# Row-tiled attention work in units of four heads of one row half, two units side by side in two sets of three PSUM banks

## The chip, the cores and the metric

The program runs on one core of a Trainium2 chip. The metric is the device time of one launch in microseconds, lower is better; the median of the runs of a kernel stands for it.

## What is computed

The reference is one pre-norm transformer block in float32 over S = 2048 rows of width D = 640: causal attention with 32 heads of width 20 over a window of 256 keys, an output projection with a residual, then a gated feed-forward of width 1536 with a residual.

```python
qkv = layernorm(x) @ wqkv                       # 32 heads, Dh = 20
scores = einsum("bhqd,bhkd->bhqk", q, k) * Dh ** -0.5
mask = (i - j >= 0) & (i - j < 256)
p = softmax(where(mask, scores, -1e9))
h = x + einsum("bhqk,bhkd->bhqd", p, v) @ wo
h2 = h + (gelu(layernorm(h) @ w_gate) * (layernorm(h) @ w_up)) @ w_down
```

## The kernel before

**Tiling.** The rows are cut into 16 blocks of 128, two blocks to a chunk for the q and k projections. A block's window is at most three key blocks: the one two blocks back (only keys later than the query's place in it count), the one before it (all), and its own (only keys up to the query). The float32 products of the projections are made of three float16 products (high by high, high by low, low by high). Scores are made twice. First q·k with the query on the output's partitions gives each row's maximum (`maxima`, 60 contraction rows; `max_out`). The maxima go back into two more contraction rows of qT (`max_rows`, `max_transpose`), and the second product with the key on the partitions (`scores`, 62 rows) comes out with the maximum subtracted, ready for the exponential (`score_out`) and for the product with v (`value_lane`).

**Row tiling.** 60 or 62 contraction rows fill less than half of TensorE's 128 rows. qT and kT hold one head of a pair on partitions 0 to 63 and the other on 64 to 127 (`par`), and a matmul on each half is issued as a pair. In the page the queries' product is `ra` or `rb` <- kT,qT and the keys' product is `ra` or `rb` <- qT,kT. The value product is column tiled: four heads in four groups of 32 output columns, into one bank that is held throughout (`pv`).

**PSUM.** The eight banks are five rings: two banks `mm` for all dense products, two `ra` and two `rb` for the row-tiled work, one `pv`, one `tp` for transposes. One step of `row_lane` takes one pair of heads of the maxima into one ring and one pair of the scores into the other, or only one of the two where the other is not ready (`row_need`, `two`). Each bank then has its own reader: VectorE reads a head's 128x384 scores with the mask added and takes the maximum (`tensor_tensor_reduce`, the custom instruction `junk` <- `ra`,`mask`, followed by a read of the accumulator into `mxs`), ScalarE takes the exponential of a head's 128x384 into `pt`. When four heads of `pt` are there, GpSimd zeroes the masked corners with two affine selects, and the value product may run.

**Order.** All instructions are emitted in an order that the program works out while it builds itself. `Clock` holds an estimated time for each engine and each buffer, `cost` an estimated price of each instruction, and the loop at the end of `block_kernel` takes, at each moment of that clock, the first lane that can start: outputs of banks first, then transposes, then side work (layernorm, weight splitting, loads), then attention lanes and the dense lane in an order that depends on which of the two is behind. On the chip each engine runs its list in order, and waits on semaphores.

**Stages.** At the start x, wq, wk and wv are loaded by SyncE's queue, the first blocks are normalised (`x_lane`) and the weights scaled and split. The first NR = 4 blocks are turned by TensorE; the others are cast (`sph`, `spl`) and turned by a DMA transpose. The q and k of a chunk leave through DRAM (`qk_out`, `qk<-qks`) and come back in the stacked form (`stack`, `qT<-qk`, `kT<-qk`). Two constant rows of kT are filled by DMA from `big`. Dense work (`dense_lane`: `qk`, `vproj`, `wo_block`, then the first part of the feed-forward) stands between the row-tiled steps. When the last block has left attention, the feed-forward runs alone.

Of the kernel before, what the change touches and what calls it, by code (L numbers as in the profile page):

```python
# [4 lines left out]

# [5 lines left out]
F32 = mybir.dt.float32  # L11
# [10 lines left out]
P = 128  # L22
# [11 lines left out]
SWITCH = 0.095  # L34
NEG = -1.0e30
# [7 lines left out]
ME = 15  # L43
# [7 lines left out]
class Clock:  # L51
# [97 lines left out]
    def others(self, ap, eng):  # L149

        return max([0.0] + [end + self.LAT for _, e, end in self.rd.get(ap.tensor.name, ())
                            if e != eng])

    def issue(self, eng, cost, reads, writes, move=False):
# [8 lines left out]
        if move:  # L163
            self.t[eng] = start + 0.4
# [10 lines left out]
class Engine:  # L175
# [4 lines left out]
    def __getattr__(self, op):  # L180
        real = getattr(self.real, op)

        def call(*args, **kw):
# [5 lines left out]
            if op in ("memset", "affine_select"):  # L189
                ins = out if op == "affine_select" else []  # L190
            self.clock.issue(self.name, self.cost(op, out[0], ins), ins, out,
                             op.startswith("dma_start"))
# [4 lines left out]
    def cost(self, op, out, ins):  # L197
# [20 lines left out]
        if self.name == "vector":  # L218
            m = max([n] + [i.free_size() for i in ins])
            if op == "tensor_copy" and half or op == "tensor_scalar" and m > 320:  # L220
                return (0.065 if half else 0.185) + 0.00053 * m
# [12 lines left out]
def block_kernel(ctx: ExitStack, tc: tile.TileContext, x, wqkv, wo, wg, wu, wd, out):  # L234
# [10 lines left out]
    banks = dict(mm=2, ra=2, rb=2, pv=1, tp=1)  # L245
# [3 lines left out]
    def bank(name, dt=F32):  # L249
        opened[name] += 1  # L250
        return nc.tile(psum, [P, 512 if dt == F32 else 1024], dt, name, banks[name])

    def ps_tp(dt=F32):
        return bank("tp", dt)

    def done(name):
        opened[name] -= 1
# [10 lines left out]
    NR = 4  # L268
# [5 lines left out]
    LEAD, TARGET = 20, 0.0  # L274
# [5 lines left out]
    def need(*reads, slots=(), when=None, eng="tensor"):  # L280

        def f():
            if when and not when() or any(opened[n] >= banks[n] for n in slots):
                return INF
            return max([nc.ready(reads, eng)]
                       + [nc.slot(psum, n, banks[n]) for n in slots])
# [28 lines left out]
    class Weight:  # L315
# [34 lines left out]
        def scale(self, lane, tp="tp"):  # L350
# [22 lines left out]
            done(tp)  # L373
# [99 lines left out]
    def transpose_part(src, hi, lo, c0, c1, tp="tp"):  # L473
# [10 lines left out]
        done(tp)  # L484
# [5 lines left out]
    def products(n, term, ready=None, at_=None):  # L490
# [5 lines left out]
        def start(i):  # L496
            if ready and not ready(i) or not ps and opened["mm"] >= banks["mm"]:
                return INF
            t = nc.ready([x for ab in term(i) for x in ab], "tensor")
            return t if ps else max(t, nc.slot(psum, "mm", banks["mm"]))  # L500
# [17 lines left out]
    def ff_scales(fg):  # L518
# [6 lines left out]
        nc.vector.tensor_tensor(ffk[:, fg, 3:4], pw[:, us:us + 1], pw[:, gs:gs + 1], op=ALU.mult)  # L525

    def ff_scales_down(fg):
        ds_ = C_D + fg
        nc.vector.tensor_scalar(ffk[:, fg, 2:3], ffk[:, fg, 3:4], pw[:, ds_:ds_ + 1],
                                _pow2(-WE - XE - UE - WE - WE), op0=ALU.mult, op1=ALU.mult)  # L530

# [13 lines left out]
    mask = wp.tile([P, 3 * P], F32, name="mask")  # L545
    nc.gpsimd.memset(mask, 0.0)
    nc.gpsimd.affine_select(mask[:, 0:P], mask[:, 0:P], pattern=[[1, P]], compare_op=ALU.is_ge,
                            fill=NEG, base=-1, channel_multiplier=-1)
# [794 lines left out]
```

## Time and profile before

| | |
|---|---|
| runs | 1103.23, 1106.27, 1107.80 us; median 1106.27 |
| span of the profiled execution, first to last instruction | 1095.7 us |
| around it (median of the runs minus the span) | 10.6 us |
| busy: TensorE / VectorE / ScalarE / GpSimd | 1023.9 / 662.5 / 452.0 / 176.4 us |
| mean granted TensorE clock over the span | 0.975 |

The profiled execution has no time of its own beside its span; 10.6 us is what the runs' median lies above it, and is taken as what surrounds the span. In a row of the trace the first number is the start or the group's busy time, as the sentence ahead of it says; PE is TensorE (PEld its weight loads), DVE VectorE, ACT ScalarE, POOL GpSimd, SP SyncE. All instructions carry the line of one helper (L184 before, L192 in the changed kernel), so they are told apart by their tiles. Matmul durations contain the pipeline's depth; their pace is read from start to start.

### The profile page before, as it was taken

The page shows a single profiled execution, that of the slowest core. Times are in us where ns is not written, and L with a number is a line of the kernel's source. Part 1 is how long each engine was busy: PE and PEld are TensorE (multiplying, and loading weights), DVE is VectorE, ACT ScalarE, POOL GpSimd, SP SyncE. Part 2 cuts the span into 40 slices and gives each one's busy share as a digit, 9 for nine tenths or more (in the row PEclk, how much of TensorE's full clock was granted, in tenths as well). Part 3 has the DMA queues.
Part 4 walks back from the last instruction along what each step waited for, and adds up shares of the span by engine and source line. Part 5 has one row for each costly group of instructions (what it writes and reads, how often), then busy time and mean ns, then how long its engine had stood idle before and what let it go on. Part 6 is the DMA issues. An engine that isn't in the chain of part 4 may idle for free.

```text
span 1095.7 us, 24693 instructions
## 1 busy us (share of the span) xinstructions
PE 1023.9 (93%) x9902; PEld 611.4 (56%) x9902; DVE 662.5 (60%) x1949; ACT 452.0 (41%) x860; POOL 176.4 (16%) x286
## 2 busy tenths in 40 slices
PE   5469899899899999999999999999999999999998
PEld 3335556566566666666554564455455555545546
DVE  8667898788686776766679739942522263222323
ACT  3213555566555766656667773411210111110110
POOL 1001112233233333323332320000000000000000
PEclk9779899899999999999999999999999999999999
DMA  6546739446253251322442114410400040001001
GB/s 240 142 91 145 205 106 203 99 97 141 63 131 90 66 128 53 94 76 70 87 150 87 42 40 154 121 25 36 109 1 1 3 124 19 1 1 49 1 1 48
DMA packets 122774, 91.41 MB, mean 83 GB/s; under 512 B 65636, under 2 KB 101732, under 8 KB 121700
## 3 DMA queue, kind: packets, MB, share of 16 engines
q1 hardware_dynamic: 99556, 79.09, 28.1%
q10 hardware_dynamic: 23104, 10.75, 3.8%
q8 instruction: 77, 1.26, 0.5%
q14 instruction: 37, 0.30, 0.1%
HBM read 54.07 MB, written 20.97 MB: 68 GB/s over the span
## 4 chain that ended last, share of the span: by engine, by line
PE 73%; DVE 9%; DMA 8%; ACT 4%; issue 3%; ACTq 1%; SPq 1%; POOL 0%; DVEq 0%; POOLq 0%
PE mm L184 58%; PE pv L184 6%; PE rb L184 4%; DVE junk L184 4%; PE ra L184 4%; ACT pt L184 3%; DMA qk<-qks 3%; DMA kT<-qk 2%; PE tp L184 1%; DMA xh<-sph 1%; DMA ol<-spl 1%; DVE am L184 1%; ACTq L184 1%; DMA xt<-in_x_dram 1%; DVE qks L184 1%
## 5 line engine op out<-in xcount | busy, mean ns | idle before, releaser
L184 POOL TENSOR_SCALAR_AFFINE_SELECT pt<-pt 128x512 f32<-128x512 f32 x240 | 154.4, 666 | 387.1 <-ACT pt L184 384.6
L184 DVE CUSTOM_DVE_ANT_0 junk<-ra,mask 128x384 bf16<-128x384 f32 (+2 forms) x260 | 136.9, 527 | 61.3 <-PE ra L184 40.5
L184 ACT ACTIVATE pt<-ra,esc 128x384 f32<-128x384 f32 (+2 forms) x260 | 131.9, 560 | 90.6 <-PE ra L184 75.5
L184 DVE CUSTOM_DVE_ANT_0 junk<-rb,mask 128x384 bf16<-128x384 f32 (+2 forms) x252 | 134.5, 534 | 57.4 <-PE rb L184 33.1
L184 ACT ACTIVATE pt<-rb,esc 128x384 f32<-128x384 f32 (+2 forms) x252 | 128.0, 560 | 79.3 <-PE rb L184 63.8
L184 DVE SCALAR_TENSOR_TENSOR gel<-mm,ffk,gel 128x512 f32<-128x512 f32 x48 | 36.0, 749 | 143.7 <-PE mm L184 143.6
L184 ACT ACTIVATE gel<-mm,ffk 128x512 f32<-128x512 f32 x48 | 33.0, 687 | 190.9 <-PE mm L184 190.9
L184 PE MATMUL pv<-pt,v 128*21 128x128 f32 x2880 | 106.4, 279 | 1.6 <-ACT oT L184 1.5
L184 DVE SCALAR_TENSOR_TENSOR ht<-mm,ffk,ht 128x320 f32<-128x320 f32 x96 | 52.8, 550 | 81.9 <-PE mm L184 81.8
L184 PEld LDWEIGHTS <-ah 128*128 128x128 f16 x768 | 74.9, 98 | 31.0 <-issue 0.4
L184 ACT CAST ah<-gel 128x512 f16<-128x512 f32 x48 | 29.7, 618 | 131.0 <-DVE gel L184 131.0
L184 PEld LDWEIGHTS pv<-pt,v 128*21 128x21 f32 x2880 | 69.4, 101 | 17.6 <-ACT oT L184 2.5
L184 PEld LDWEIGHTS <-qT 60*128 60x128 f16 x640 | 27.1, 93 | 92.4 <-issue 84.6
L184 PEld LDWEIGHTS <-kT 62*128 62x128 f16 x1440 | 60.9, 96 | 31.8 <-issue 20.7
L184 PEld LDWEIGHTS <-gu 128*128 128x128 f16 x480 | 45.6, 98 | 53.5 <-issue 1.2
L184 PE MATMUL mm<-hTh,gu 128*128 128x512 f16 x240 | 71.9, 379 | 0.0
L184 PE MATMUL rb<-kT,qT 60*128 60x384 f16 (+2 forms) x312 | 46.0, 298 | 20.0 <-DMA kT<-qk 16.6
L184 PE MATMUL mm<-w2h,xh 128*128 128x320 f16 x160 | 49.0, 306 | 12.6 <-DVE qks L184 12.6
L184 PE MATMUL mm<-xh,w0h 128*128 128x256 f16 x200 | 56.8, 284 | 1.8 <-ACT w0h L184 1.8
L184 PE MATMUL mm<-xh,w1h 128*128 128x256 f16 x200 | 56.1, 280 | 2.5 <-DVE qks L184 2.5
L184 PE MATMUL mm<-xh,w0l 128*128 128x256 f16 x200 | 56.5, 282 | 1.0 <-DVE w0l L184 1.0
L184 PE MATMUL mm<-xl,w0h 128*128 128x256 f16 x200 | 56.6, 283 | 0.0
(212 smaller groups left out, 2254.0 us busy)
## 6 DMA issues: line engine op xcount, KB each, us to landing
qk<-qks ACTq DMA_DIRECT2D x64, 128.0 KB
qT<-qk SPq DMA_DIRECT2D x48, 160.0 KB
kT<-qk SPq DMA_DIRECT2D x48, 160.0 KB
ht<-in_x_dram SPq DMA_DIRECT2D x16, 320.0 KB
h_dram<-ht SPq DMA_DIRECT2D x16, 320.0 KB
ht<-h_dram SPq DMA_DIRECT2D x16, 320.0 KB
out_dram<-ht SPq DMA_DIRECT2D x15, 320.0 KB
xt<-in_x_dram SPq DMA_DIRECT2D x13, 320.0 KB
```

The lines of the kernel that those rows point to most:

```text
L184: r = real(*args, **kw)
```

## The change

**Units.** The unit of row-tiled work becomes four heads of one row half (`heads(u)`): twelve matmuls of 128x128 for a block with three key blocks, where the maxima's before were one of 384 (or 256 and 128, where the ring of kT wraps) for each head. A step of `row_lane` takes two units of different halves, a maximum unit and a score unit, or two of a kind, and `zip_longest` issues their matmuls in turn: one of the one half, one of the other. Each unit has a set of three PSUM banks, banks 0 to 2 and 3 to 5; within a set bank t holds key block t of all four heads. A step begins only when both sets are quiet (`row_need`, `set_time`).

**Readers.** A score unit has one exponential of 128x1536. A maximum unit of three key blocks has two VectorE instructions: a predicated copy of 128x512, which puts the own block's scores over those of the oldest block where the own block is allowed (the two blocks' allowed keys complement each other), and one maximum over the remaining 128x1024 to four numbers. With fewer key blocks the mask is added to the own block instead of the copy. The accumulator reads and `junk` are gone.

**Banks.** One PSUM tile `ps8` (named `ps_73` in some lists) replaces the rings. Bank 6 is for dense products and transposes, bank 7 is `pv`. `pick` lends banks of a set to dense products or transposes only while at most one of the two queues of row-tiled work has anything (for a transpose: while it can keep one set for rows); a set with a bank lent out holds up the next step.

**Start.** NR becomes 8: blocks 2 to 7 are loaded two to a `pt` buffer, between the loads of wq, wk and wv, and all of the first eight blocks are turned by TensorE. The two DMAs of constants into kT become twelve GpSimd memsets (`const_lane`), for which `stack` waits. LEAD becomes 10. The columns of wv and the rows of wo are reordered on the host so that a unit's four heads lie together. After the last value product bank 7 is free for dense work, and from then on no set is held back.

**The order.** TensorE, in the middle of the attention stage, before: one step of row-tiled work (a pair of maxima, three pairs of scores), then a unit's value product (`pv`), a transpose of the values' output (`oT`) and dense work (`w3h`).

```order
L184 LDWEIGHTS qT
L184 MATMUL ra<-kT,qT 128x384
L184 LDWEIGHTS qT
L184 MATMUL ra<-kT,qT 128x384
L184 LDWEIGHTS kT
L184 MATMUL rb<-qT,kT 128x128
...
L184 MATMUL pv<-pt,v_104 21x128 x4
L184 MATMUL pv<-pt,v_103 21x128 x4
L184 MATMUL pv<-pt,v_105 21x128 x4
L184 MATMUL tp<-ident,oT 128x117 x4
L184 LDWEIGHTS ol
L184 MATMUL mm<-w3h,ol 128x320
```

Now, at such a place: the end of a step of twelve pairs, a unit's value product, a transpose, and the next step.

```order
L192 LDWEIGHTS qT
L192 MATMUL ps_73<-kT,qT 128x128
L192 LDWEIGHTS kT
L192 MATMUL ps_73<-qT,kT 128x128
L192 MATMUL ps_73<-pt,v_107 21x128 x4
L192 MATMUL ps_73<-pt,v_106 21x128 x4
L192 MATMUL ps_73<-pt,v_108 21x128 x4
L192 MATMUL ps_73<-ident,oT 128x117 x4
L192 LDWEIGHTS qT
L192 MATMUL ps_73<-kT,qT 128x128
L192 LDWEIGHTS kT
L192 MATMUL ps_73<-qT,kT 128x128
```

Over the whole list the stretches of row-tiled matmuls fall from 282 to 128, those of value products from 128 to 124, and the changes between full, row and column tiling from 686 to 415. Between the 128 steps stands more or less of other work; in 37 of the 127 gaps it is at most a value product with six dense matmuls, or thirteen dense matmuls alone.

VectorE, before: four heads' maxima are four custom instructions, each with its accumulator read (`mxs`).

```order
L184 ISA junk,mxs<-rb,mask 128x384
L184 ISA mxs 128x1
L184 ISA junk,mxs<-ra,mask 128x384
L184 ISA mxs 128x1
L184 ISA junk,mxs<-ra,mask 128x384
L184 ISA mxs 128x1
L184 RECIPROCAL rec<-tp 128x16
L184 TENSOR_TENSOR o_5473<-tp,rec 128x320
```

Now two units' maxima, with the split of a block's output (`spl`) between the copy and the maximum of the first, and a layernorm (`lyah` to `lxn`) between the units.

```order
L192 COPY_PREDICATED ps_73<-tri,ps_73 128x512
L192 TENSOR_TENSOR spl<-o_2563,sph 128x640
L192 TENSOR_REDUCE mxs<-ps_73 128x4
L192 SCALAR_TENSOR_TENSOR lyah<-lyh,lveh 128x1
L192 TENSOR_SCALAR lyah<-lyah 128x1
L192 TENSOR_TENSOR lyh<-lyh,lyah 128x1
L192 TENSOR_SCALAR lxn<-ht,lmvh,lyh 128x640
L192 COPY_PREDICATED ps_73<-tri,ps_73 128x512
L192 TENSOR_REDUCE mxs<-ps_73 128x4
```

512 custom instructions and as many reads became 112 copies and 128 maxima; 28 of the copies have one or two other instructions between them and their maximum.

SyncE's queue near the start, before: the constants, weight slices of wo, the stacked q and k of the first chunk, and then DMA transposes of x.

```order
L184 DMA kT<-big 2x96x128 x2
L184 DMA wsl<-in_wo_dram 128x640 x3
L184 DMA qT<-qk_225 20x4096 x6
L184 DMA xt<-in_x_dram 128x640 x2
L184 DMA kT<-qk_349 20x16x256 x6
L184 DMA_TRANSPOSE xh<-sph 128x5x128
L184 DMA_TRANSPOSE xl<-spl 128x5x128
```

Now the stacked q and k of two chunks come one after the other, with no transpose ahead of them.

```order
L192 DMA pt<-in_x_dram 128x640 x2
L192 DMA wsl<-in_wo_dram 128x640 x3
L192 DMA qT<-qk_229 20x4096 x6
L192 DMA kT<-qk_353 20x16x256 x6
L192 DMA xt<-in_x_dram 128x640 x2
L192 DMA qT<-qk_819 20x4096 x6
L192 DMA kT<-qk_925 20x16x256 x6
```

**The diff, cut to its core.**

```diff
-    banks = dict(mm=2, ra=2, rb=2, pv=1, tp=1)
+    ps8 = psum.tile([P, 8 * 512], F32, name="ps8")
+    SETS = ((0, 1, 2), (3, 4, 5))
+    MM, PV = 6, 7
...
+    def pick(kind):
+        want = (len(maxq) > 0) + (len(scoreq) > 0) - (kind == "tp")
+        lent = {s for s in (0, 1) if any(held.get(b) in ("mm", "tp") for b in SETS[s])}
+        can = [MM]
+        if pos["over"]:
+            can.append(PV)
+        for s in (0, 1):
+            if not any(held.get(b) == "row" for b in SETS[s]) and 2 - len(lent | {s}) >= want:
+                can.extend(SETS[s])
...
-    NR = 4
+    NR = 8
-    LEAD, TARGET = 20, 0.0
+    LEAD, TARGET = 10, 0.0
...
+    def heads(u):
+        return u % 2, range(4 * (u // 2), 4 * (u // 2) + 4)
...
+        for c, pr in enumerate(prs):
+            for i, kb in enumerate(ks, 3 - len(ks)):
+                yield v[:, i, c, :], b.c.qT[rs, pr, b.cols], kT[rs, pr, kb % RK, :]
...
     def row_need():
+        t2 = max(set_time(0), set_time(1))
+        if t2 == INF or not maxq and not scoreq:
+            return INF
...
+            for ops in zip_longest(*gens):
+                for op in ops:
+                    if op:
+                        nc.tensor.matmul(*op, start=True, stop=True)
...
-        nc.vector.tensor_tensor_reduce(junk[:, :n * P], ps[:, :n * P], mask[:, (3 - n) * P:], 1.0,
-                                       -3.0e38, ALU.add, ALU.max,
-                                       b.mx[:, par * 16 + pr:par * 16 + pr + 1])
+        if n == 3:
+            nc.vector.copy_predicated(v[:, 0], tri4, v[:, 2])
+            w = v[:, 0:2]
...
+        nc.vector.tensor_reduce(mx, w.rearrange("p t c k -> p c t k"), axis=AX.XY, op=ALU.max)
...
-        nc.scalar.activation(pt[:, 2 * (pr % 2) + par, :n, :], ps[:, :n, :], AF.Exp,
-                             scale=esc)
+        nc.scalar.activation(pt[:, 3 - n:], v, AF.Exp, scale=esc)
...
-        nc.sync.dma_start(kT[64 * par + 60:64 * par + 62].rearrange("p i r n -> p (i r) n"),
-                          big[0:2, None, :].to_broadcast([2, RK * H // 2, P]))
+                nc.gpsimd.memset(kT[64 * par + 32:64 * par + 64, :, r, :], _pow2(ME))
...
-        if i:
-            load_x(i + 1)
+        load_x(2 * i + 2)
+        load_x(2 * i + 3)
```

More of the change, by code (lines that the diff above doesn't have):

```diff
@@ L282, in f @@
         def f():
-            if when and not when() or any(opened[n] >= banks[n] for n in slots):
+            if when and not when():
                 return INF
-            return max([nc.ready(reads, eng)]
-                       + [nc.slot(psum, n, banks[n]) for n in slots])
+            return max([nc.ready(reads, eng)] + [room(n) for n in slots])
         return f
@@ new lines, in scores @@
+    def scores(j, u, banks):
+        b = B[j]
+        par, prs = heads(u)
+        rs = slice(64 * par, 64 * par + 62)
+        v = set_view(banks)
+        ks = window(j)
+        b.pt[u] = at("pt", [P, 3, 4, P], F32, 3)
+        pos["units"] += 1
+        for i, kb in enumerate(ks, 3 - len(ks)):
+            for c, pr in enumerate(prs):
+                yield v[:, i, c, :], kT[rs, pr, kb % RK, :], b.c.qT[rs, pr, b.cols]
+        tasks.append(score_out(j, u, banks, b.pt[u]))
+        pos["score"] += 1
@@ L915, in normalise @@
                                 rec[:, :, None].to_broadcast([P, 16, DH]), op=ALU.mult)
-        done("tp")
+        done(t)
+        pos["over"] = j == NB - 1 and half
         if half:
```

324 lines of the change are left out of this document (176 added, 148 removed).

## The prediction

> **What bounds the kernel now.** I read the page's busy shares and its chain first, then the busy times by stage, then the timeline of one steady stretch.
>
> ```profile
> PE 1023.9 (93%) x9902; PEld 611.4 (56%) x9902; DVE 662.5 (60%) x1949; ACT 452.0 (41%) x860; POOL 176.4 (16%) x286
> PE 73%; DVE 9%; DMA 8%; ACT 4%; issue 3%; ACTq 1%; SPq 1%; POOL 0%; DVEq 0%; POOLq 0%
> ```
>
> TensorE is busy for 93% of the span and carries 73% of the chain that ended last. An edit pays here only if it takes time out of TensorE's own list or out of its waits. The stages, with the columns stretch, PE, PEld, DVE, ACT and POOL busy (instructions), granted clock, DMA share, GB/s:
>
> ```profile
> 0.00:110.00 110.00, 69.75 (x528) 45.20 (x529) 78.68 (x276) 31.62 (x63) 10.09 (x26) 0.89 0.56 155
> 110.00:301.00 191.00, 174.99 (x2148) 112.19 (x2147) 154.11 (x506) 111.43 (x231) 49.32 (x76) 0.95 0.57 131
> 301.00:642.00 341.00, 329.94 (x4689) 207.76 (x4688) 244.39 (x792) 222.41 (x438) 108.56 (x170) 0.98 0.35 87
> 642.00:1096.00 454.00, 449.20 (x2544) 246.21 (x2540) 185.33 (x377) 86.58 (x132) 8.49 (x14) 1.00 0.15 43
> ```
>
> TensorE idles for 40 us in the first 110 us, 16 us up to 301, 11 us up to 642 and 5 us in the feed-forward after that. VectorE is at 72 to 81% in the first three stages, so it is the second bound. The steady stretch on TensorE (start, duration; what follows x is the count):
>
> ```profile
> 443.07 0.85 PE L184 MATMUL pv<-pt,v 128*21 128x128 f32 x24
> 443.86 0.24 PE L184 MATMUL tp<-ident,m 128*64 128x128 f16 x1
> ...
> 444.18 0.30 PE L184 MATMUL mm<-w2h,xh 128*128 128x320 f16 x1
> 444.32 0.30 PE L184 MATMUL mm<-w2l,xh 128*128 128x320 f16 x1
> 444.55 0.34 PE L184 MATMUL rb<-kT,qT 60*128 60x384 f16 x2
> 444.72 0.33 PE L184 MATMUL ra<-qT,kT 62*128 62x128 f16 x6
> 444.99 0.31 PE L184 MATMUL mm<-w2h,xl 128*128 128x320 f16 x1
> ...
> 446.08 0.30 PE L184 MATMUL mm<-w2l,xh 128*128 128x320 f16 x1
> 446.22 0.30 PE L184 MATMUL mm<-w2h,xl 128*128 128x320 f16 x1
> 446.45 0.34 PE L184 MATMUL rb<-kT,qT 60*128 60x384 f16 x2
> ```
>
> A dense matmul takes 0.14 us from start to start. Between the last dense one and a row-tiled step lie 0.23 us (444.32 to 444.55, and 446.22 to 446.45), so 0.095 us goes into the change of tiling, and no wait for a bank is visible on top. The pair of maxima takes 0.17 us, the three pairs of scores 0.27 us with the change back, so 0.17 without it: 0.055 us for a pair of 128 columns in both products. A unit's value product takes 0.79 us with its change, about 0.7 without.
>
> **The change part by part.**
>
> *Row-tiled matmuls: nothing.* Three pairs of 128 replace one pair of 384, at 3 x 0.055 = 0.165 against 0.17 us. The extra weight loads lie beside the other half's matmul, as they do for the scores now. The total stays at 1440 pairs x 0.055 = 79 us.
>
> *Fewer changes of tiling: -26 us.* The order has 415 instead of 686; 271 x 0.095 = 25.7 us, all on TensorE's list.
>
> *The readers.* Two maxima of one step on VectorE, and the nearest rows to the new instructions (here the first number is the group's busy time, the second the mean in ns):
>
> ```profile
> 443.11 0.55 DVE L184 CUSTOM_DVE_ANT_0 junk<-ra,mask 128x384 bf16<-128x384 f32 x1
> 443.58 0.08 DVE L184 DVE_READ_ACCUMULATOR2_ANT mxs<- 128x1 f32 x1
> 443.81 0.56 DVE L184 CUSTOM_DVE_ANT_0 junk<-ra,mask 128x384 bf16<-128x384 f32 x1
> 444.29 0.08 DVE L184 DVE_READ_ACCUMULATOR2_ANT mxs<- 128x1 f32 x1
> ```
>
> ```profile
> L184 DVE SCALAR_TENSOR_TENSOR gel<-mm,ffk,gel 128x512 f32<-128x512 f32 x48 | 36.0, 749 | 143.7 <-PE mm L184 143.6
> L184 DVE TENSOR_TENSOR al<-gel,ah 128x512 f16<-128x512 f32 x48 | 33.0, 688 | 21.2 <-ACT ah L184 21.2
> L184 DVE TENSOR_REDUCE am<-wst 128x1 f32<-128x512 f32 x20 | 12.8, 674 | 0.0
> L184 DVE TENSOR_REDUCE am<-wst 128x1 f32<-128x640 f32 x12 | 9.6, 814 | 0.1
> L184 ACT ACTIVATE pt<-ra,esc 128x384 f32<-128x384 f32 x228 | 120.3, 581 | 76.2 <-PE ra L184 63.7 <-POOL pt L184 7.0 <-PE mm L184 3.1
> L184 ACT ACTIVATE pt<-rb,esc 128x256 f32<-128x256 f32 x18 | 7.5, 471 | 7.9 <-PE rb L184 5.7 <-DVE lyxb L184 2.2
> ```
>
> One head's maximum occupies VectorE for 0.70 us (443.11 to 443.81), four heads for 2.8. The new maximum over 1024 is 674 + 512 x (814 - 674)/128 = 1.23 us. No row shows a predicated copy. From below it is the 512-element row with one operand from PSUM less, 0.69 us; from above, if mask, data and the old values are read in two passes, the price of 1024 elements, 1.23 us. I take 0.73, between the two 512-element rows, because it writes as many elements as they do. With 0.04 us between the two a unit costs 2.0 us, 0.8 less than now, over 112 units 90 us less on VectorE. The exponential of 1536 is 581 + 1152 x (581 - 471)/128 = 1.57 us against 4 x 0.58 = 2.32: 84 us less on ScalarE. Neither is on the path by itself.
>
> *A wait for both sets: +34 us.* A step now holds six banks, and the next one waits until VectorE and ScalarE have emptied all of them. Behind that wait in TensorE's list stand the step, the value product and all dense matmuls, and ScalarE and VectorE wait for these. How soon VectorE starts after a matmul, and TensorE after VectorE:
>
> ```profile
> 444.92 0.56 DVE L184 CUSTOM_DVE_ANT_0 junk<-rb,mask 128x384 bf16<-128x384 f32 x1 [0.54 <-PE rb L184]
> ...
> 67.86 0.08 DVE L184 DVE_READ_ACCUMULATOR2_ANT mxs<- 128x1 f32 x1
> 68.00 0.21 PE L184 MATMUL ra<-kT,qT 60*128 60x128 f16 x1 [0.25 <-DVE mxs L184]
> ```
>
> The maximum starts 0.03 us after the pair's end (444.55 + 0.34), and TensorE goes on 0.06 us after the read's end. So from one step's start to the next: 0.61 (the twelfth pair starts) + 0.21 (its duration) + 0.03 + 2.0 + 0.06 = 2.9 to 3.0 us. The step itself is 0.66, so the gap must hold 2.3 us of other work. I priced the list's 127 gaps by the rows above (0.14 a dense matmul of 320, 0.11 of 256, 0.66 the value product, 0.4 four transposes, 0.095 a change): 51 hold less, 37 of them under 1.7 us, and the shortfalls sum to 34 us. At a unit price of 1.8 us (a needed gap of 2.1) it would be 25 us; with the copy at 1.23, or with one more 512-element instruction ahead of the maximum (needed 2.9), 75 us. ScalarE's path, 1.57 us, is shorter and hides below. In the stretch shown today's pair of maxima needs 1.4 us of VectorE and the dense work between the steps covers it, which is why no such wait is to be seen.
>
> The Trainium skill speaks against the change here: TensorEngine Tiling (Array Packing), section PSUM Bottleneck, says that tiling speeds up TensorE but not the emptying of PSUM, which may become the limit. By that rule the sum would be the row of the +75 us; the trace so far agrees with the direction only (TensorE needs 0.34 us for what VectorE empties in 1.4).
>
> *One bank for dense work: +4 us.* While both queues are filled only bank 6 serves dense products. The order puts a row step or a value product behind most group ends, at least 0.75 us; 16 ends have only one step. If each lacks 0.5 us it is 8; I take half, since some lie in gaps already counted. Bounds 0 and 20.
>
> *The start: -20 us.*
>
> ```profile
> 104.43 4.11 DMA xh<-sph
> ...
> 108.62 0.04 ACT sph L184
> ...
> 110.08 0.51 ACT pt L184 x2
> ```
>
> ```profile
> 107.39 0.28 PE L184 MATMUL ra<-kT,qT 60*128 60x256 f16 x2
> 110.38 0.47 PE L184 MATMUL rb<-qT,kT 62*128 62x128 f16 x2 [2.71 <-ACT pt L184]
> ```
>
> ScalarE's queue waits there for a DMA transpose before it can cast the next block, the exponential stands behind it, and TensorE loses 2.71 us. For blocks 4 to 7 these transposes go to TensorE (four blocks, 20 matmuls, 2 us). Ahead of the first row step the list now has 36 us of TensorE work instead of 19, while TensorE idles 40 us in that stage. I take 12 us back of the 40 (0 to 25), and 8 of the 16 idle us and of the 5% of missing clock (10 us) in the second stage (0 to 20). Against it stand the moved loads and the memsets:
>
> ```profile
> GB/s 240 142 91 145 205 106 203 99 97 141 63 131 90 66 128 53 94 76 70 87 150 87 42 40 154 121 25 36 109 1 1 3 124 19 1 1 49 1 1 48
> ...
> L184 POOL MEMSET mask<- 128x384 f32 x1 | 0.4, 418 | 0.3 <-POOLq L1330 0.3
> L184 POOL MEMSET big<- 128x128 f16 x1 | 0.2, 206 | 0.0
> ```
>
> At 240 GB/s two x blocks ahead of wk are 2.7 us, three ahead of wv 4 us. Twelve memsets of 2048 elements at 206 + 1920 x (418 - 206)/256 ns are 1.8 us each, 22 us on a GpSimd that works 10 us in 110, beside the scaling of the weights; a layernorm's GpSimd step can stand 1.8 us behind one. Both are in the 12. Should the cover fail they cost up to 6 us.
>
> *The feed-forward: -3 us* of its 5 idle us, since seven and then eight banks serve it instead of two.
>
> Sum: 1095.7 - 26 + 34 + 4 - 20 - 3 = 1085 us of span; with the 10.6 us that the runs' median lies above the span, 1095 us, 1.0% less. With the bounds that lie near (25 to 45 us of shortfall, 10 to 30 at the start) 1077 to 1106. A measurement of this kernel can tell about 0.5%, 5.5 us, from no change.
>
> **The rivals.**
>
> *The sets come free later (slower).* For it: 28 copies have another VectorE instruction ahead of their maximum, and the copy's price is unknown. At a needed gap of 2.9 us the shortfall is 75 instead of 34: 1095 + 41 = 1136 us. It decides from a shortfall of 51 us, a needed gap of 2.6 us. Against it: 37 of the short gaps are fixed by the order, and VectorE has 90 us less to do. Chance 0.27.
>
> *VectorE's and ScalarE's relief is worth more (faster).* At 81% VectorE also delays the outputs of dense groups. If the start gives 40 of its 76 us (40 + 16 idle, and 10 each of clock) and the shortfall is 25: 1095 - 20 - 9 = 1066 us. Against it: most of the idle time at the start is loads and the way through DRAM, which stay. Chance 0.18.
>
> *The clock drops in the short gaps (slower).*
>
> ```profile
> 472.80:476.30 3.50, 1.76 (x32) 1.05 (x34) 2.27 (x9) 0.89 (x3) 0.00 (x0) 0.99 0.16 47
> 476.30:479.70 3.40, 3.40 (x37) 1.67 (x26) 0.68 (x4) 1.28 (x4) 1.23 (x2) 0.50 0.01 3
> 547.90:551.30 3.40, 2.41 (x49) 1.18 (x41) 2.51 (x10) 2.34 (x5) 1.23 (x2) 0.99 0.15 56
> ```
>
> A stretch with TensorE 50% busy was followed by one at half clock; one with 71% was not. In a short gap TensorE would work 2.1 of 3.0 us, 70%. If half of the 37 run at half clock, each is 1.2 us longer: +22 us, 1117 us. The Trainium skill names this in TensorE: Matmul & The Clock Gate, section A second HAM failure mode: psum-queue depth-cycling: short idle times between groups of matmuls that cycle through banks make the clock swing. The trace has drops only behind emptier stretches. Chance 0.05.
>
> *The halves do not overlap when one runs a maximum and the other a score (slower).* The pairs now seen are of one product. 79 us more: 1174 us. The two halves share nothing that the equal pairs do not; chance 0.04.
>
> **How the numbers follow.** My forecast has 0.46; most of its own spread lies below 1100.7 us, 0.33, some within half a per cent, 0.11, a little above, 0.02. Faster: 0.33 + 0.18 = 0.51. Same: 0.11 + 0.04 of the first rival's near end = 0.15. Slower: 0.02 + 0.23 + 0.05 + 0.04 = 0.34. The likeliest value is 1095. The range goes from 1056, ten below the faster rival, to 1138, just past the first slower one; the forecast's own is 1088 to 1117 with the 10.6 us.
>
> **What would show it.** A copy of 0.7 and a maximum of 1.2 us; steps 2.9 to 3.0 us apart where little stands between them, and there the wait for VectorE in the row list of TensorE; 0.095 us at each change, 0.66 us for a full step; DVE near 570, ACT near 370 us; less idle time ahead of 301 us. The forecast falls if TensorE's waits for the sets pass 51 us, if a step takes over 0.8 us, or if the first 110 us idle as before.

## The result and the profile after

The changed kernel takes 1149.57 us (median, 1145.12 to 1152.97), the kernel before beside it 1104.75: a ratio of 1.041, 95% interval 1.037 to 1.046. It is slower, and outside the predicted range. The span of its profiled execution is 1151.0 us. The engines' busy times and the shares of the chain that ended last:

```profile
PE 1009.4 (88%) x10722; PEld 642.7 (56%) x10722; DVE 636.6 (55%) x1185; ACT 386.8 (34%) x480; POOL 195.3 (17%) x298
PE 68%; DVE 14%; DMA 9%; ACT 4%; issue 3%; SPq 1%; ACTq 1%; POOL 0%; DVEq 0%
```

TensorE works 14.5 us less (1009.4 against 1023.9) and idles 141.6 us instead of 71.8. VectorE has 14% of the chain instead of 9%. By the granted clock in the two traces, half clock took 28.8 us of TensorE's busy time instead of 17.6 (an estimate: a busy microsecond at a clock of 0.50 counts as half a microsecond of work). Without it the work fell from 1006.2 to 980.6 us. So the spans' difference of 55 us is made of 69.8 us more idle time, 11.2 more of half clock, and 25.6 less work. By stage (stretch, PE, PEld, DVE, ACT, POOL busy, granted clock, DMA share, GB/s):

```profile
0.00:110.00 110.00, 84.47 (x677) 64.47 (x678) 85.09 (x202) 32.84 (x61) 30.25 (x37) 0.96 0.59 169
110.00:301.00 191.00, 156.66 (x2599) 113.47 (x2598) 152.47 (x277) 96.51 (x111) 55.94 (x87) 0.95 0.50 115
301.00:642.00 341.00, 275.59 (x4361) 196.20 (x4357) 194.90 (x287) 144.09 (x151) 86.25 (x138) 0.93 0.35 82
642.00:1152.00 510.00, 492.63 (x3097) 268.55 (x3095) 204.18 (x422) 113.37 (x159) 22.86 (x36) 0.99 0.15 42
```

The start gained: 25.5 us idle instead of 40.3. The second stage lost it again (34.3 instead of 16.0), and the third lost most: 65.4 instead of 11.1, at a clock of 0.93 instead of 0.98. The last value product of attention ends at 698 us instead of 645, and what follows it takes 453 us instead of 451: the loss lies in attention. The new instructions (busy, mean ns of one, then idle time before them):

```profile
L192 ACT ACTIVATE pt<-ps,esc 128x1536 f32<-128x1536 f32 x112 | 171.4, 1539 | 164.2 <-PE ps L192 150.4 <-POOL pt L192 12.4 <-DVE qks L192 1.0
L192 DVE TENSOR_REDUCE mxs<-ps 128x4 f32<-128x1024 f32 x120 | 145.7, 1218 | 2.5
L192 DVE COPY_PREDICATED ps<-tri,ps 128x512 f32<-128x512 int32 x112 | 77.1, 692 | 94.9 <-PE ps L192 94.8
```

What TensorE waited for, the kernel before (us in total, times, the longest):

```profile
PE rb L184 <- DMA kT<-qk: 16.6, 6, 4.5
PE mm L184 <- DVE qks L184: 15.3, 4, 12.6
...
PE ra L184 <- DMA kT<-qk: 5.2, 2, 4.5
PE ra L184 <- DVE mxs L184: 2.4, 7, 0.6
PE mm L184 <- DMA ol<-spl: 2.3, 4, 0.9
```

And the changed kernel:

```profile
PE ps L192 <- DVE mxs L192: 29.0, 32, 2.3
PE ps L192 <- DMA kT<-qk: 25.0, 4, 8.0
...
PE ps L192 <- ACT v L192: 10.1, 11, 2.3
PE ps L192 <- DVE qks L192: 9.0, 11, 2.2
PE ps L192 <- DMA oh<-sph: 8.7, 3, 3.6
PE ps L192 <- ACT oT L192: 5.9, 8, 2.2
PE ps L192 <- DVE ht L192: 5.5, 6, 1.3
PE ps L192 <- DMA ol<-spl: 5.4, 4, 2.2
PE ps L192 <- ACT mT L192: 4.9, 5, 1.1
```

Three things grew most. The wait for the maxima (`mxs`), which is the wait for the sets, is 29.0 us. The instructions that empty the bank of dense products and transposes (`v`, `qks`, `ht`, `mT`) are waited for 10.1 + 9.0 + 5.5 + 4.9 = 29.5 us; before only `qks` stands high, with 12.6 of its 15.3 us in one wait of the start. (`oT` is another matter: ScalarE copies it out of bank 7, and those who wait for it are value products and the transposes that read it.) And `oh`, `ol`, the turned inputs of the output projection, come late, 14.1 us instead of 2.5. The wait for kT hardly grew: 25.0 us in 4 waits, against 21.8 us in 8 before.

The wait for the sets is the loop that the prediction described. A piece of the chain (start, duration):

```profile
309.16 0.88 PE ps L192 x24
310.03 0.70 DVE ps L192
310.75 1.24 DVE mxs L192
312.03 0.88 PE ps L192 x24
312.90 0.70 DVE ps L192
313.62 1.24 DVE mxs L192
314.90 0.88 PE ps L192 x24
```

Step, copy, maximum, next step: 2.87 us from 309.16 to 312.03, and 2.87 again.

The other one, on the timeline between two steps (start, duration, engine, and in brackets the idle time ahead and who ended it):

```profile
503.16 0.85 PE L192 MATMUL ps<-pt,v 128*21 128x128 f32 x24
503.38 1.54 ACT L192 ACTIVATE pt<-ps,esc 128x1536 f32<-128x1536 f32 x1 [1.54 <-PE ps L192]
503.95 0.31 PE L192 MATMUL ps<-w2h,xl 128*128 128x320 f16 x1
...
504.82 0.43 ACT L192 ACTIVATE v<-ps 128x320 f32<-128x320 f32 x1
...
505.30 0.30 PE L192 MATMUL ps<-w2h,xh 128*128 128x320 f16 x1 [1.04 <-ACT v L192]
```

The last matmul of a dense sum starts at 503.95. The bank that it fills is emptied by ScalarE's `v`, which stands behind the exponential of 1.54 us. The next dense sum needs the same bank and waits 1.04 us. Where dense work runs without row steps, each sum pays:

```profile
383.70 0.27 PE L192 MATMUL ps<-xh,w1h 128*128 128x256 f16 x1 [2.17 <-DVE qks L192]
...
388.53 0.27 PE L192 MATMUL ps<-xh,w1l 128*128 128x256 f16 x1
390.21 0.27 PE L192 MATMUL ps<-xh,w1h 128*128 128x256 f16 x1 [1.41 <-DVE qks L192]
...
391.74 0.27 PE L192 MATMUL ps<-xh,w1l 128*128 128x256 f16 x1
392.94 0.30 PE L192 MATMUL ps<-w3h,oh 128*128 128x320 f16 x1 [0.93 <-DVE qks L192]
...
395.07 0.34 PE L192 MATMUL ps<-kT,qT 60*128 60x128 f16 x5
402.60 1.22 PE L192 MATMUL ps<-kT,qT 60*128 60x128 f16 x19 [7.19 <-DMA kT<-qk]
```

The products with `w1h` and `w1l` are the three k sums of a chunk. They wait 2.17 and 1.41 us for the bank between them, and the sum behind them (`w3h`) 0.93. The last of the k products starts at 391.74, and 3.3 us later a row step starts that stops in its middle for 7.19 us, until k is back from DRAM. The k sums had lost 3.6 us to the bank, half of that stop. So late dense work can come back as a wait for kT. The value products of block 7 (counted from 0) end at 369 us, 20 us earlier than before (390); those of block 8, the first of the next chunk, at 434, 9 us later (425).

### The profile page after: what moved, and what is told of

Read it like the earlier page. It is cut to its first block, busy times and chain, and to the rows that moved or that the text cites. A ratio compares the mean times of both kernels' runs of the same rounds, so it can differ in the third digit from the quotient of the medians.

```text
span 1151.0 us, 24750 instructions
## 1 busy us (share of the span) xinstructions
PE 1009.4 (88%) x10722; PEld 642.7 (56%) x10722; DVE 636.6 (55%) x1185; ACT 386.8 (34%) x480; POOL 195.3 (17%) x298
## 4 chain that ended last, share of the span: by engine, by line
PE 68%; DVE 14%; DMA 9%; ACT 4%; issue 3%; SPq 1%; ACTq 1%; POOL 0%; DVEq 0%
PE ps L192 68%; DVE mxs L192 4%; DVE ps L192 2%; ACT pt L192 2%; DMA kT<-qk 2%; DVE am L192 2%; DMA qk<-qks 1%; DMA qT<-mT 1%; DMA xh<-sph 1%; DMA ol<-spl 1%; SPq L192 1%; DVE qks L192 1%; ACTq L192 1%; DMA xl<-spl 1%; DVE ht L192 1%
## 5 line engine op out<-in xcount | busy, mean ns | idle before, releaser
L192 ACT ACTIVATE pt<-ps,esc 128x1536 f32<-128x1536 f32 (+2 forms) x128 | 185.8, 1459 | 186.3 <-PE ps L192 166.1
L192 DVE TENSOR_REDUCE mxs<-ps 128x4 f32<-128x1024 f32 (+1 forms) x128 | 150.8, 1185 | 2.5
L192 PE MATMUL ps<-kT,qT 60*128 60x128 f16 x1440 | 101.1, 223 | 54.6 <-DVE mxs L192 27.9
L192 DVE COPY_PREDICATED ps<-tri,ps 128x512 f32<-128x512 int32 x112 | 77.1, 692 | 94.9 <-PE ps L192 94.8
L192 PEld LDWEIGHTS <-qT 60*128 60x128 f16 x1440 | 82.0, 97 | 55.5 <-issue 50.7
L192 PE MATMUL ps<-pt,v 128*21 128x128 f32 x2880 | 105.6, 278 | 3.7 <-ACT oT L192 2.4
L192 PE MATMUL ps<-qT,kT 62*128 62x128 f16 x1440 | 98.1, 221 | 3.1 <-DMA qT<-mT 1.7
L192 PEld LDWEIGHTS ps<-pt,v 128*21 128x21 f32 x2880 | 68.9, 101 | 23.9 <-issue 5.5
L192 PE MATMUL ps<-hTh,gu 128*128 128x512 f16 x240 | 71.9, 379 | 0.0
L192 PE MATMUL ps<-xh,w0h 128*128 128x256 f16 x200 | 56.9, 284 | 6.4 <-ACT w0h L192 1.9
L192 PE MATMUL ps<-xh,w1l 128*128 128x256 f16 x200 | 56.2, 281 | 1.9 <-DVE w1l L192 1.8
```

Source lines behind the costliest of these rows:

```text
L192: r = real(*args, **kw)
```

## The experiments

**Theories.** D: one bank for dense products and transposes, emptied behind long readers, is what costs. S: the sets, held by VectorE's round of copy and maximum, cost. O: the order places steps ahead of loads that land later. N: any new order of the work costs as much, by luck. And the start: gain or cost. All ratios are to the kernel before beside them, with 95% intervals.

**One dense bank in the kernel before** (`b_mm1`).

```diff
-    banks = dict(mm=2, ra=2, rb=2, pv=1, tp=1)
+    banks = dict(mm=1, ra=2, rb=2, pv=1, tp=1)
```

> The kernel before with one bank instead of two for dense products (the other one is left unused; transposes keep theirs); the order is worked out anew. Three theories of the 45 us that the change costs. S, the sets: a step waits until VectorE has gone through three banks in 2 us, and all of TensorE's list waits behind it. D, the dense bank: dense products and transposes have one bank and wait until it is emptied behind the long readers of the sets. O, the order: steps stand ahead of DMAs that land later than the list was built for. D expects 15 to 35 us more than before, with TensorE waiting for the readers of dense banks (qks, v, ht). S and O expect within 5 us of before, as my forecast did with its 4 us.

Measured 1496.94 us, ratio 1.356 (1.353 to 1.358), far above every forecast. Its waits:

```profile
PE mm L184 <- DVE ht L184: 73.4, 107, 2.5
PE mm L184 <- DVE gel L184: 41.7, 43, 1.9
PE mm L184 <- ACT gel L184: 41.4, 47, 1.9
```

Much of it is feed-forward, which the changed kernel spares by using the sets' banks there; but attention too ends 186 us later (831 against 645). Divided by their counts these waits are 0.7 to 1.0 us each.

**The changed kernel without the copy** (`a_nocopy`), every engine in its old order.

```diff
-            nc.vector.copy_predicated(v[:, 0], tri4, v[:, 2])
...
-        nc.vector.tensor_reduce(mx, w.rearrange("p t c k -> p c t k"), axis=AX.XY, op=ALU.max)
+            nc.vector.real.tensor_reduce(mx, v[:, :, :, 0:86].rearrange("p t c k -> p c t k"),
+                                         axis=AX.XY, op=ALU.max)
```

> The changed kernel with its instruction order kept, but without the predicated copy; the maximum reads 86 of 128 keys of each of the three blocks instead (1032 elements), so the masking of the maxima and some keys are left out of them. VectorE's round for a unit falls from 2.0 to 1.3 us. S expects TensorE's waits for VectorE's maxima to fall from 29 us to below 8 and the time by 20 to 30 us, to 1120 to 1130 us. D expects 5 to 10 us less, since dense banks are also emptied a little sooner behind VectorE. O expects no more than 3 us.

Measured 1139.22 us, ratio 1.032 (1.030 to 1.034): 10 us less. The maximum still reads 1032 elements, so only the copy's 0.7 us of 2.0 is gone. The wait for the maxima fell from 29.0 to 18.8, and the waits for the dense bank stayed (`v` 10.0, `qks` 8.6). S holds a part, not the whole.

**More banks lent to dense work** (`a_lend`).

```diff
-        want = (len(maxq) > 0) + (len(scoreq) > 0) - (kind == "tp")
+        want = min(1, (len(maxq) > 0) + (len(scoreq) > 0) - (kind == "tp"))
```

> The changed kernel with one line of its bank rule changed: one set may always be lent to dense products and transposes, also while both queues of row-tiled work are filled; the order is worked out anew. D expects 10 to 30 us less (1120 to 1140 us), with the waits of dense products for v, qks and ht gone. S expects 10 us more or worse, since a step then waits for a lent bank as well. O expects within 10 us either way.

Measured 1236.16 us, ratio 1.120 (1.118 to 1.121). The wait for the maxima rose to 99.8 us: a lent bank holds up a whole step. D's forecast of a gain failed, though the waits it names did fall (`v` from 10.1 to 2.8 us); S's held. Eight banks do not hold two sets and a loan.

**The start alone in the kernel before** (`b_start`): eight early blocks two to a buffer, the new order of loads, constants by memset, and the gates that the shared buffers then need.

```diff
-    NR = 4
+    NR = 8
...
+        load_x(2 * i + 2)
+        load_x(2 * i + 3)
```

> The kernel before with the start of the changed one alone: eight blocks loaded early and turned by TensorE, constants of kT by GpSimd memsets; a score unit also waits until the x blocks in its buffer are used, and a chunk's q and k until both of its blocks are ready. My forecast's term for the start expects 10 to 20 us less than before, 1085 to 1095 us. O expects that the start only moves work ahead that is then missing at later chunk changes: within 5 us of before.

Measured 1125.36 us, ratio 1.020 (1.018 to 1.023): 22 us more, where a gain was expected.

**The changed kernel with the old start** (`a_start4`): the same edit undone.

> The changed kernel with the start of the kernel before: four early blocks of x instead of eight, each in an own buffer, the old order of the first loads, and the constants of kT by DMA instead of by memsets; the order is planned anew. If the start part costs in the changed kernel what it cost by itself in the kernel before (22 us), this gives 1125 to 1132 us. If the loss lies in the sets, the dense bank or the order at chunk changes, the start is no part of it: 1145 to 1165 us, with the idle time of TensorE in the first 110 us back from 25 us to 35 to 40 us.

Measured 1171.50 us, ratio 1.064 (1.059 to 1.068): 22 us more too, above both forecasts, and TensorE idles 32.4 us in the first 110 instead of 25.5. In the changed kernel the start is a gain, though no larger than what one number of the planner moved (25 us, below).

**Loads expected later** (`a_dma`).

```diff
-            end = self.moved[eng] + 1.7
+            end = self.moved[eng] + 3.7
```

> The changed kernel with one number of the planner changed: a DMA is expected to land 3.7 us after its transfer instead of 1.7 us, so that what needs it is placed later. Theory O (steps stand ahead of loads that land later): the 25 us of waits for kT and most of the 14 us for oh and ol go, and 1120 to 1135 us remain. Theories S (sets held by VectorE's round) and D (one bank for dense work): the waits only change their name, 1143 to 1157 us.

Measured 1164.94 us, ratio 1.058 (1.054 to 1.063). The wait for kT fell from 25.0 to 8.1 us and the one for the maxima rose from 29.0 to 50.7. The edit also holds up the start: block 0's value products end at 188 us instead of 140, and from there to block 15's it makes up 37 of the 47 us. So it does not decide on O by itself. `a_z` below says more: with one dense bank its wait for kT is only 3.8 us, and it still takes 1148 us. The loss is therefore not the wait for kT. With two dense banks that wait falls to 13.3, 7.0 and 4.2 us; how much of the 25.0 us late dense work made is not shown beyond the one place above, and the waits for `oh` and `ol` (19.3 us in `a_z`) were not tried apart.

**Dense work kept further ahead** (`a_tgt`): TARGET 0.6 instead of 0.0.

> The changed kernel with dense work kept 0.6 of a block further ahead of attention (TARGET 0.6 instead of 0.0); the order is planned anew. Theory O (attention outruns the dense work and then has no q and k at chunk changes): 1120 to 1138 us, with blocks 8, 12 and 14 ending earlier. Theory S: 1145 to 1155 us, nothing changes in the steps. Theory D: 1150 to 1170 us, since more dense work in a row waits for its own one bank.

The number never decides: the lists of all engines came out the same. So this is the changed kernel once more, 1147.23 us against 1149.57, ratio 1.041 (1.037 to 1.045). It tells nothing about O, only that two measurements of one kernel lie 2.3 us apart.

**A shorter exponential** (`a_exp`), every engine in its old order.

```diff
-        nc.scalar.activation(pt[:, 3 - n:], v, AF.Exp, scale=esc)
+        nc.scalar.real.activation(pt[:, 2], v[:, n - 1], AF.Exp, scale=esc)
```

> The changed kernel, every engine in its old order, with ScalarE's exponential over one of the three key blocks only (128 x 512 instead of 128 x 1536); all three value products of a head read that one block. Two thirds of the exponentials are left out. Theory D (the dense bank is emptied behind long readers): the waits for ScalarE's copies (v 10.1, oT 5.9, mT 4.9 us) fall by half or more and the whole is 10 to 20 us shorter, 1130 to 1140 us. Theory S: the exponential ends well before the maxima's VectorE round, which holds the step: 0 to 5 us shorter. Theory O: no change.

Measured 1136.43 us, ratio 1.031 (1.025 to 1.037): 13 us less, where S and O expected at most 5. The step's loop goes over VectorE and does not contain the exponential, and the wait for the maxima did not fall (30.7 us). The copies of ScalarE's queue came sooner: `v` 8.4, `mT` 1.9 and `oT` 3.1 us instead of 10.1, 4.9 and 5.9. The time is D's, but `v` did not fall by half, these waits are 7.5 of the 13 us, and `oT` empties bank 7. So ScalarE's long instruction costs, and this run does not say how much of it through the dense bank.

**A second dense bank** (`a_pv1`, `a_2mm`). All eight banks are taken, so room is made in bank 7: a unit's value products use 128 of its 512 columns and ScalarE copies them out after each unit. The control stops there; `a_2mm` gives the other 384 columns to dense sums that fit.

```diff
-        if pos["over"]:
+        if pos["over"] or cols <= 384:
             can.append(PV)
...
+        if b == PV and not pos["over"]:
+            ap = ap[:, 128:512]
...
-                nc.scalar.copy(oT, pv)
+            nc.scalar.copy(oT[:, u % 4, :], pv)
```

> The control for the next two: the changed kernel, in which the value products of a unit use one quarter of their bank, 128 columns, and ScalarE copies them out after each unit (128 copies of 128 x 128 instead of 32 of 128 x 512); the three free quarters are left unused and dense work still has its one bank. The order is planned anew. Both theories D and S: no gain, 1145 to 1190 us, since values wait for one more copy.

> As the control, but the three free quarters (384 columns) serve dense work as a second bank wherever a product has at most 384 columns (v, the output projection, half of k and q); no unit's value products run while a dense sum is open there. Planned anew. Theory D (one bank for dense work and transposes is what costs): 30 to 60 us below the control and 25 to 45 below the changed kernel, 1105 to 1125 us, and the waits for the copies that empty the dense bank fall below half. Theory S (the sets held by VectorE's round): within 15 us of the control, 1135 to 1175 us.

One line separates the two: a dense product may take the free columns. The control: 1171.97 us, ratio 1.063 (1.059 to 1.067). With the second bank: 1122.91 us, ratio 1.019 (1.014 to 1.025), 49 us below the control and 27 below the changed kernel. Its waits:

```profile
PE ps L192 <- DVE mxs L192: 22.3, 23, 3.0
...
PE ps L192 <- DMA kT<-qk: 13.3, 5, 4.9
PE ps L192 <- ACT oT L192: 13.2, 26, 1.7
```

`v`, `ht` and `mT` are no longer among the larger ones, and kT's wait fell with them (the control had `v` 13.8, `ht` 5.9, kT 20.2). So did the wait for the maxima, from 31.3 to 22.3: part of what S counts is gone with the bank too. `oT` is dearer than it was, the price of the room: value products and dense sums, half each, wait there for ScalarE's copy. D holds, within all its bounds; S said less than 15 us from the control.

**The same with another planner's number** (`a_2mmff`: FFPREP 0.3, how far ahead the later layers' weights are prepared) **and that number alone** (`a_ff`).

> The kernel with the second dense bank and one number of the planner changed (FFPREP 0.3 instead of 0.2: how far ahead the weights of the later layers are prepared). Only another order of the same work: theory D says 1090 to 1125 us, near the run without it; should it differ by more than 20 us from that, the luck of the order is as large as the effect that is looked for.

> The changed kernel, one dense bank, with only the planner's number changed that the faster of the two-bank kernels had (FFPREP 0.3). If the bank is what brought that kernel to 1098 us (theory D): 1138 to 1155 us. If it was the order (theory N): 1115 to 1130 us.

Two banks: 1098.21 us, ratio 0.996 (0.994 to 0.998). One bank: 1142.67 us, ratio 1.037 (1.033 to 1.042). The difference is 44 us, the bank's again, and the wait for the maxima is 23.1 us against 34.0. But the number alone moved the two-bank kernel by 25 us, more than the 20 that I had named as the bound of the order's luck, and the one-bank kernel by 7.

**A new order of the kernel before** (`b_late`: LATE 0.5 instead of 0.4).

> The kernel before with one number of the planner changed (LATE 0.5 instead of 0.4: how far ahead side work is issued), so that the same work stands in another order. Theory N (the loss is only the luck of a new order): this too moves by 20 us or more, to 1120 or above. Theories D and S: within 15 us of the kernel before, 1090 to 1118 us.

Measured 1098.75 us, ratio 0.997 (0.995 to 1.000). Against N, for the kernel before.

**VectorE's round with two dense banks** (`a_2f_nocopy`: the edit of `a_nocopy` in `a_2mmff`, old order).

> The faster kernel with two dense banks, every engine in its old order, without VectorE's copy of a max unit and with its maximum over 86 of 128 keys of each block. The copy and part of the maximum are left out. Theory S still holds a part of the time: the 23 us of waits for the maxima fall to about 10, 1083 to 1092 us. If VectorE's round costs nothing more than its own waits are worth: 1093 to 1100 us.

Measured 1092.92 us, ratio 0.991 (0.988 to 0.994): 5 us less, the wait for the maxima 14.6 instead of 23.1 us. It lies at the border of the two forecasts: what is left of S in the copy is small.

**The old start with two dense banks** (`a_2f_start4`).

> The faster kernel with two dense banks, with the start of the kernel before (four early blocks of x, the old order of loads, the constants by DMA), planned anew. If the start of the change is a gain of its own: 1112 to 1125 us. If it is a cost, as it was by itself in the kernel before: 1075 to 1090 us. If its sign hangs on the plan and not on the start: 1093 to 1108 us.

Measured 1140.71 us, ratio 1.033 (1.027 to 1.039): the start of the change is worth 42 us here, planned anew, more than any of the three forecasts.

**The fastest version, and its numbers alone** (`a_2z`, `a_z`, `b_z`): AHEAD 0.25, PREP 0.4, RAMPMAX 0.15, FFPREP 0.25, LATE 0.5, and values taken as soon as one unit waits; with two dense banks, with one, and in the kernel before.

> Two dense banks and another set of the planner's numbers (AHEAD 0.25, PREP 0.4, RAMPMAX 0.15, FFPREP 0.25, LATE 0.5, values taken at one waiting unit instead of two). Theory D: 1088 to 1102 us, near the faster two-bank kernel, whatever the exact order, and so at or a little below the kernel before.

> The changed kernel, one dense bank, with the planner's numbers of the fastest version. Theory D: 1140 to 1170 us, since the numbers do not help where the bank is missing. Theory N (the order's luck): 1095 to 1125 us.

> The kernel before with the planner's numbers of the fastest version. Theory D: 1095 to 1115 us, since it had two dense banks before and those numbers only reorder it. If the numbers themselves are the gain: 1075 to 1085 us.

Two banks: 1078.25 us, ratio 0.978 (0.974 to 0.981), the fastest of all. One bank: 1148.28 us, ratio 1.040 (1.035 to 1.046). The kernel before: 1104.40 us, ratio 1.003 (1.000 to 1.005). The numbers bring nothing without the bank; with it the difference is 70 us. A place in `a_2z` like that of the 1.04 us wait above (the same products, `w2h` and `w2l`):

```profile
379.99 1.54 ACT L192 ACTIVATE pt<-ps,esc 128x1536 f32<-128x1536 f32 x1
380.03 0.30 PE L192 MATMUL ps<-w2h,xl 128*128 128x320 f16 x1
...
380.26 0.85 PE L192 MATMUL ps<-pt,v 128*21 128x128 f32 x24
...
381.05 0.31 PE L192 MATMUL ps<-w2h,xh 128*128 128x320 f16 x1
...
381.42 0.43 ACT L192 ACTIVATE v<-ps 128x320 f32<-128x320 f32 x1
```

The copy `v` stands behind the exponential as before, at 381.42, but the next dense sum has begun at 381.05, with no wait, in the other bank.

## Why the prediction was wrong, point by point

**The step that failed: one bank for dense work, +4 us with bounds 0 and 20.** Three comparisons price that bank at 49 us (1171.97 to 1122.91, one line apart), 44 (1142.67 to 1098.21) and 70 us (1148.28 to 1078.25); in the last two the one-bank kernel also keeps bank 7 whole for values. Each is planned anew, and each is larger than the 25 us that a number of the planner alone moved. In the profiled executions of the three pairs 33, 30 and 44 us of the difference are idle time of TensorE, and 3, 13 and 19 us half clock. Against the changed kernel itself, with its own numbers, the bank and the room made for it together gave 27 us, and 1.9% above the kernel before remained. The prediction took "at least 0.75 us" of other work behind a group's end as cover and asked for 0.5 us at 16 ends. It priced the reader of the bank and forgot the queue ahead of that reader: the exponential of 1.54 us on ScalarE, copy and maximum of 1.9 us on VectorE, both started by the step that was meant to be the cover. It left out what happens where dense work stands alone (2.17 and 1.41 us between the k sums above), and the return of the delay (there half of a stop of 7.19 us, and 3.4 us at half clock). The direct waits for the bank's readers, 29.5 us, are thus less than the bank's price. The Trainium skill has the rule that the prediction lacked, in Perfetto Trace Analysis, section Optimizing Tensor Performance: "Independent matmul groups should rotate through different PSUM banks so the ACT/DVE evacuation of one overlaps the next group's matmuls". The two timelines agree: 1.04 us of waiting with one bank, none with two.

**Fewer changes of tiling, -26 us: right in size.** TensorE's busy time is only 14.5 us lower, but without the half clock its work is 25.6 us lower in the changed kernel, and 26.3 and 28.5 in `a_2mmff` and `a_2z`. Other differences of its list, such as the transposes of four more blocks, are in these numbers. **Row-tiled matmuls, nothing:** right; the twelve pairs of a step start 0.056 us apart (309.16 to 309.77 in the loop above), also where one half runs a maximum and the other a score, as there, so the rival without overlap falls.

**The readers: sizes right, sum wrong.** 0.692, 1.218 and 1.54 us against 0.73, 1.23 and 1.57. But VectorE's busy time is 636.6 us, not 570: the 0.70 us per head was the distance from start to start, and only 0.557 of it is busy time, the measure of the 662.5 us from which the 90 were taken. Four heads were 2.23 us of busy time, so a unit saves 0.32, not 0.8: over 112 units 36 us, not 90. ScalarE's busy time is 386.8 us, not near 370. Whether VectorE's idle 0.15 us between two maxima was of use to other work was not tried.

**The wait for both sets, +34 us: right** as a wait, 29.0 us, in the described loop of 2.87 us. Taking 0.7 us from each round gave back 10 us, and 5 with two dense banks. So the rival that came nearest in time, the sets that come free later (1136 us), had the wrong mechanism: in the changed kernel the waits for the sets are 29.0 us, not the 51 at which it decides. The Trainium skill's rule that the emptying of PSUM may become the limit (TensorEngine Tiling (Array Packing), section PSUM Bottleneck) was right in kind: 29.0 + 29.5 of the 141.6 idle us stand behind VectorE's and ScalarE's reads of PSUM. It struck at the bank beside the tiled work as much as at the tiled work's own.

**The start, -20 us: right in sign in this kernel.** Undone, it costs 22 us, and 42 with two dense banks; the first 110 us idle 14.7 us less, where I took 12. In the second stage, where I took 8 us back, TensorE idles 18 us more: there it waits 13.5 us for the maxima, 1.0 before, and 9.8 for the readers of the dense bank, 0.2 before. The 22 us lie within what an order alone can move, the 42 do not. Why the start costs 22 us in the kernel before stays open; its gates for the shared buffers are not in the changed kernel, and they were not tried apart.

**The feed-forward, -3 us: nothing.** From 66% of the dense matmuls, when attention is over in both kernels, to the last the trace gives 290.8 us in both (801.3 to 1092.1, and 856.5 to 1147.3).

**The frame.** The 10.6 us around the span were mostly the spread between runs: the profiled run of the changed kernel took 1152.97 us for a span of 1151.0. Hence the spans differ by 55 us and the medians by 45.

**The rival of the clock: wrong mechanism.** In the loop of short gaps the clock stayed at full speed; its drops follow emptier stretches (below). They cost 11 us more than before, half of the 22 that the rival named.

What stays open besides: how far a given order is luck. One number moved the two-bank kernel by 25 us, and each of the three prices of the bank may contain such a share.

## What to carry to other kernels

Before a buffer is taken from a side stream to widen the main one, add up, at the shared bank, the queue ahead of its reader and not only the reader: one long instruction in place of four short ones frees the main work's banks no later, and the side stream's bank stands behind all of it. A second bank for the side stream was worth more here (44 to 70 us) than every saving of the wider units (26 us of changes of tiling). And busy time is not pace: a saving that is to be taken from an engine's busy time has to be measured in durations, not in the distance from one start to the next.

## What the hardware showed besides

In these traces the granted clock falls after largely idle stretches, not in the loop's short gaps. Stretches of the changed kernel (columns as in the stages): a round of the loop; a wait of 8 us, what follows, and the stretch after that; then 3.4 us with the wait of 2.17 us shown above, and what follows.

```profile
309.00:312.00 3.00, 2.28 (x52) 1.65 (x52) 2.03 (x3) 1.54 (x1) 0.36 (x2) 1.00 1.61 120
322.40:330.40 8.00, 0.00 (x0) 0.01 (x1) 0.00 (x0) 0.00 (x0) 0.00 (x0) 0.57 0.34 63
330.40:334.00 3.60, 3.58 (x31) 2.27 (x33) 1.96 (x3) 2.15 (x2) 0.62 (x2) 0.54 0.00 0
334.00:337.50 3.50, 3.50 (x75) 2.49 (x76) 2.70 (x3) 2.71 (x3) 2.26 (x4) 1.00 0.99 88
...
381.47:384.88 3.41, 1.25 (x12) 1.06 (x11) 2.18 (x3) 0.60 (x1) 0.00 (x0) 1.00 0.83 204
384.88:388.30 3.42, 3.42 (x18) 2.43 (x17) 0.00 (x0) 0.00 (x0) 0.00 (x0) 0.50 0.06 15
```

At 75% busy the loop keeps a clock of 1.00. After the 8 us of waiting the next 3.6 us run at 0.54, which loses another 1.7 us, and then the clock is back. The shorter wait was enough too: 3.4 us at 37% busy were followed by 3.4 us at 0.50. In the third stage the clock was 0.93 in the changed kernel, 0.95 in `a_2mm`, 0.98 in `a_2z` and 0.99 in `a_2mmff`, in the order of TensorE's idle time there (65.4, 40.6, 37.6 and 31.4 us).

The predicated copy of 128 x 512 with its data in PSUM took 0.692 us, between the 0.688 and 0.749 us of the two 512-element rows of the prediction: the 1.23 us that a second pass over mask, data and old values would have cost was not to be seen.
